# SwiGLU feed-forward on one core: the first loads in one line on SyncE, and two token chunks projected ahead of the third's transposes

## The chip, the core and the metric

The kernel runs on one core of a Trainium2 chip. The metric is the device time of one execution in microseconds (us), lower being better. A core has engines that run their own instruction streams side by side: TensorE (PE, matrix products), VectorE (DVE), ScalarE (ACT), GpSimd (POOL) and SyncE (SP), which here does nothing but issue transfers. Transfers between the device memory (HBM) and the on-chip memory are issued by SyncE and ScalarE, one queue each, and are carried by 16 DMA engines. Engines wait for one another, and for transfers, through semaphores.

## What is computed

```python
def reference(x, w_gate, w_up, w_down):
    g = _silu(x @ w_gate)
    u = x @ w_up
    return (g * u) @ w_down
```

`x` is 1 x 2048 x 640, `w_gate` and `w_up` are 640 x 1536, `w_down` is 1536 x 640, all bfloat16.

## The kernel before, in words

Tokens are worked on in four blocks of 512 (`S_BLK`), each of four chunks of 128. For each block the kernel forms the gate and up projections transposed, features on partitions: for each of the 12 slices of 128 features (`fc`) and for gate and up in turn, five matmuls (one per 128 of the 640 inputs) add up in a PSUM tile of 128 x 512 (`proj`, line 190). ScalarE applies silu to the gate tile, VectorE multiplies it with the up tile into `aT` (`gate`, line 208). Then the block is multiplied with `w_down` (lines 260 to 314) and stored.

The projections need `x` transposed (`xT`). For blocks 1 to 3 transposing DMAs bring it (`turn_x`). Block 0 can't wait for that: its four chunks x0 to x3 are loaded as they lie (`load_x`, line 83) and transposed by TensorE against an identity, five 128 x 128 transposes a chunk, and copied from PSUM into `xT` by VectorE, or by ScalarE and VectorE in two parts (`transpose_chunk`, line 178; `split`, line 224).

The weights come in column chunks, `W_CHUNKS` (line 44): feature slice 0, slice 1, slices 2 and 3, then 4 to 7 and 8 to 11 (`load_w`, line 80). A row of slice 0 is 256 bytes in memory. Lines 106 to 119 set the order of the first loads:

- SyncE: x0, x1, the last two fifths of gate slice 0, the last three of up slice 0, gate slice 1, x3, up slice 1, gate 2-3, up 2-3, and so on.
- ScalarE: x2, the first three fifths of gate slice 0, the first two of up slice 0, then the first activation (`silu_first`, line 114), with which its table is loaded.

A queue's issues go out in order, and an issue that waits holds up those behind it. The program uses eight completion semaphores for all these transfers, in turn; a transfer that takes one again waits for the transfer that had it before.

The order of TensorE's work at the start is written out in `head` (line 217): 18 filler matmuls (`warm`), transposes of chunks 0 and 2, two fillers, transposes of chunk 1, two fillers, then the projections of feature slices 0 and 1 over the first three chunks (`pg0`, `pu0`, `pg1`, `pu1` are gate and up of slices 0 and 1), with the transposes of chunk 3 before `pu1`, and last the four small projections of chunk 3. `outer_chunks` (line 200) picks chunks 0 and 2 out of a PSUM tile and of `xT`, so that one matmul of 256 columns covers both. `keep_order` holds TensorE, ScalarE, VectorE and SyncE to the written order. After the head the loop over blocks (line 247) goes on with feature slice 2 of block 0.

Of the kernel before, what the change touches and what calls it, by code (L numbers as in the profile page):

```python
# [10 lines left out]
def _body(  # L11
# [8 lines left out]
    nc = tc.nc  # L20
    P = nc.NUM_PARTITIONS
# [11 lines left out]
    KD = D // P  # L33
# [6 lines left out]
    N_WARM, N_GAP = 18, 2  # L40
# [3 lines left out]
    W_CHUNKS = [(0, 1), (1, 2), (2, 4), (4, 8), (8, 12)]  # L44
# [12 lines left out]
    wg_sb = consts.tile([P, KD, F], bf16)  # L57
    wu_sb = consts.tile([P, KD, F], bf16)
# [14 lines left out]
    wg_v = w_gate.rearrange("(kd p) f -> p kd f", p=P)  # L73
    wu_v = w_up.rearrange("(kd p) f -> p kd f", p=P)
    wd_v = w_down.rearrange("(kf p) d -> p kf d", p=P)

    def wslice(a, b):
        return slice(a * P, b * P)

    def load_w(eng, dst, src, a, b):  # L80
        eng.dma_start(out=dst[:, :, wslice(a, b)], in_=src[:, :, wslice(a, b)])

    def load_x(eng, c0, c1):
        eng.dma_start(out=x_sb[:, c0:c1, :], in_=x_v[:, c0:c1, :])  # L84
# [11 lines left out]
    def keep_order(engine):  # L96

        traced = [i for i in nc.cur_bb.bb.instructions if i.engine == engine]
        for a, b in zip(traced, traced[1:]):
            issue_order(a, b)  # L100
# [4 lines left out]

    load_x(nc.sync, 0, 1)
    load_x(nc.scalar, 2, 3)
    load_x(nc.sync, 1, 2)
    for dst, src, k in ((wg_sb, wg_v, 3), (wu_sb, wu_v, 2)):
        for eng, k0, k1 in ((nc.scalar, 0, k), (nc.sync, k, KD)):  # L110
            eng.dma_start(out=dst[:, k0:k1, wslice(0, 1)], in_=src[:, k0:k1, wslice(0, 1)])
    load_w(nc.sync, wg_sb, wg_v, *W_CHUNKS[1])
    load_x(nc.sync, 3, 4)
    nc.scalar.activation(silu_first[:], ones[:, 0:1], ACT.Silu)
# [12 lines left out]
    def turn_w(dst, src):  # L127
# [7 lines left out]
        out=x_row[:],  # L135
        in_=x2[S - T : S, :].rearrange("t d -> (t d)").partition_broadcast(P),
# [35 lines left out]
    def warm(n):  # L172
        for _ in range(n):
            nc.tensor.matmul(  # L174
                pw[:, 0:P], lhsT=ones[:], rhs=ones[:], start=True, stop=True
            )

    def transpose_chunk(c, parts):
        c_sl = slice(c * P, (c + 1) * P)
        for copy, tag, k0, k1 in parts:  # L180
            pt = psum.tile([P, k1 - k0, P], bf16, tag=tag, name="pt")
            for kd in range(k0, k1):
                nc.tensor.transpose(  # L183
                    out=pt[:, kd - k0, :],
                    in_=x_sb[:, c, kd * P : (kd + 1) * P],
                    identity=ident[:],
                )
            copy(out=xT[:, k0:k1, c_sl], in_=pt[:])  # L188

    def proj(ps, w_sb, fc, sb, c0, c1, cols=lambda ap: ap):  # L190
        for kd in range(KD):
            nc.tensor.matmul(  # L192
                cols(ps[:, c0:c1]),
                lhsT=w_sb[:, kd, fc * P : (fc + 1) * P],
                rhs=cols(xT[:, kd, sb * S_BLK + c0 : sb * S_BLK + c1]),
                start=(kd == 0),
                stop=(kd == KD - 1),
            )
# [4 lines left out]
    def gu_tiles():  # L203
        pg = psum.tile([P, S_BLK], f32, tag="gu", name="pg", bufs=4)
        pu = psum.tile([P, S_BLK], f32, tag="gu", name="pu", bufs=4)
        return pg, pu

    def gate(pg, pu, sb, fc, n_s):

        s0 = sb * S_BLK  # L210
        sg = work.tile([P, S_BLK], f32, name="sg")
        nc.scalar.activation(sg[:, 0:n_s], pg[:, 0:n_s], ACT.Silu)  # L212
        nc.vector.tensor_tensor(  # L213
            out=aT[:, fc, s0 : s0 + n_s], in0=sg[:, 0:n_s], in1=pu[:, 0:n_s], op=ALU.mult
        )

    def head():

        dve, act = nc.vector.tensor_copy, nc.scalar.copy
        split = [(act, "po_a", 0, 2), (dve, "po_b", 2, KD)]
        late = (SUB - 1) * P
        (pg0, pu0), (pg1, pu1) = gu_tiles(), gu_tiles()
        warm(N_WARM)
        transpose_chunk(0, [(dve, "po_a", 0, KD)])
        transpose_chunk(2, [(dve, "po_b", 0, KD)])
        warm(N_GAP)  # L230
        transpose_chunk(1, split)
        warm(N_GAP)
        proj(pg0, wg_sb, 0, 0, 0, late, outer_chunks)
        proj(pg0, wg_sb, 0, 0, P, 2 * P)
        proj(pu0, wu_sb, 0, 0, 0, late)
        proj(pg1, wg_sb, 1, 0, 0, late)
        transpose_chunk(3, split)
        proj(pu1, wu_sb, 1, 0, 0, late)
        for fc, pg, pu in ((0, pg0, pu0), (1, pg1, pu1)):
            proj(pg, wg_sb, fc, 0, late, S_BLK)  # L240
            proj(pu, wu_sb, fc, 0, late, S_BLK)
            gate(pg, pu, 0, fc, S_BLK)
        keep_order(mybir.EngineType.PE)
        keep_order(mybir.EngineType.Activation)

    head()
    for sb in range(NSB):
        n_s = S_BLK if sb < NSB - 1 else S_BLK - T
# [26 lines left out]
        for q in range(P // Q):  # L275
            nc.scalar.dma_start(
                out=out2[
                    sb * S_BLK : sb * S_BLK + n_t, DA + q * Q : DA + (q + 1) * Q
                ].rearrange("(i r) c -> r i c", r=Q),
                in_=ot_q[q * Q : (q + 1) * Q, :].rearrange("r (i c) -> r i c", c=Q),  # L280
# [110 lines left out]
def kernel(tc, *args):  # L391
    _body(tc, *args)
    tc.close()
    tc.compile()
    _trim(tc.nc)
# [30 lines left out]
```

## Time and profile before

| | us |
|---|---|
| median of 4 runs | 164.4 |
| lowest and highest | 164.17, 164.72 |
| the profiled execution: its own time | 164.72 |
| its span in the trace | 163.4 |
| TensorE busy in it (799 matmuls) | 160.3 |
| VectorE, ScalarE busy | 111.8, 42.6 |
| first matmul of feature slice 2, block 0 | 10.26 |

The first loads of the profiled execution, from the trace's issue rows (start of the issue, and us until the data have landed):

| transfer | queue | KB | issued | to landing |
|---|---|---|---|---|
| x0 | SyncE | 160 | 0.00 | 2.3 |
| x2 | ScalarE | 160 | 0.12 | 2.7 |
| x1 | SyncE | 160 | about 0.45 | 3.0 |
| gate slice 0, three fifths | ScalarE | 96 | 0.57 | 3.7 |
| gate slice 0, two fifths | SyncE | 64 | 0.91 | 3.3 |
| up slice 0, two fifths | ScalarE | 64 | 1.05 | 3.5 |
| up slice 0, three fifths | SyncE | 96 | 1.39 | 3.6 |
| gate slice 1 | SyncE | 160 | 1.90 | 4.0 |
| x3 | SyncE | 160 | 2.81 | 3.6 |
| up slice 1 | SyncE | 160 | 3.20 | 3.6 |
| gate slices 2-3 | SyncE | 320 | 4.31 | 5.9 |
| up slices 2-3 | SyncE | 320 | 4.72 | 6.5 |

All times in a trace count from the start of the span. A timeline line gives start, duration, engine, line of the kernel, what was done, the count, and in brackets how long the engine had been idle and what ended that. Matmuls run in a pipeline: a group's duration runs to the end of its last matmul, so the pace is read from start to start. The time of an execution is its span plus some 1.3 us around it.

### The profile page before, as it was taken

Reading aid. Unit: us, or ns where it says so; the run is one execution under the profiler, and the core shown is the slowest. Engines: PE = TensorE matmul, PEld = TensorE weight load, DVE = VectorE, ACT = ScalarE, POOL = GpSimd, SP = SyncE. Lnnn points to the kernel's source line nnn. Section 1 sums busy time; section 2 is a strip of 40 time slices with the busy share of each in tenths; the row PEclk is TensorE's granted clock in tenths of the full one; section 3 lists DMA queues with packets and bytes.
Section 4 is the critical chain, followed back from the end, with each engine's and each line's share of the span. In section 5 each row is a group of like instructions: output and inputs, shape, how many; then the busy total and the mean of one; then the engine's idle time right before and its main releaser. Section 6 shows DMA issues by size and latency. Waiting matters only on the chain.

```text
span 163.4 us, 2121 instructions
## 1 busy us (share of the span) xinstructions
PE 160.3 (98%) x799; PEld 76.8 (47%) x799; DVE 111.8 (68%) x251; ACT 42.6 (26%) x73; POOL 0.6 (0%) x6
## 2 busy tenths in 40 slices
PE   9989999999999999999999999999999999999994
PEld 8754444444444444444444444444444444445442
DVE  2133333399649999979919999979964999993000
ACT  3142222212142222212332222221214222222121
POOL 1000000000000000000000000000000000000000
DMA  7999999994149997002210000000420000000312
GB/s 202 246 308 353 363 234 246 226 234 65 65 107 178 230 178 147 0 0 26 72 64 0 4 0 0 2 0 0 64 68 32 0 0 0 0 4 0 51 37 72
DMA packets 42585, 15.86 MB, mean 97 GB/s; under 512 B 34512, under 2 KB 42448, under 8 KB 42576
## 3 DMA queue, kind: packets, MB, share of 16 engines
q1 hardware_dynamic: 33680, 14.88, 37.1%
q10 hardware_dynamic: 8896, 0.85, 3.8%
q8 instruction: 6, 0.10, 0.3%
q14 instruction: 3, 0.02, 0.1%
HBM read 7.21 MB, written 2.62 MB: 60 GB/s over the span
## 4 chain that ended last, share of the span: by engine, by line
PE 92%; DMA 6%; ACTq 0%; DVE 0%; issue 0%
PE pg L192 30%; PE pu L192 30%; PE po_a L288 25%; PE po_t L263 6%; DMA wg_sb<-in_w_gate_dram 6%; PE po_b L305 0%; ACTq L84 0%; DVE ot_b L313 0%
## 5 line engine op out<-in xcount | busy, mean ns | idle before, releaser
L192 PE MATMUL pg<-xT,wg_sb 128*128 128x512 bf16 (+4 forms) x255 | 60.4, 369 | 0.6 <-DMA wg_sb<-in_w_gate_dram 0.6
L192 PE MATMUL pu<-xT,wu_sb 128*128 128x512 bf16 (+3 forms) x250 | 59.9, 370 | 0.0
L213 DVE TENSOR_TENSOR aT<-sg,pu 128x512 bf16<-128x512 f32 (+1 forms) x48 | 32.7, 683 | 30.0 <-PE pu L192 28.6
L212 ACT ACTIVATE sg<-pg 128x512 f32<-128x512 f32 (+1 forms) x48 | 28.6, 596 | 68.2 <-PE pg L192 65.1
L288 PE MATMUL po_a<-wd_sb,aT 128*128 128x512 bf16 x192 | 42.1, 379 | 0.0
L145 DVE SCALAR_TENSOR_TENSOR prod<-wgT,x_row 128x640 f32<-128x640 bf16 x48 | 39.4, 821 | 1.1
L145 DVE SCALAR_TENSOR_TENSOR prod<-wuT,x_row 128x640 f32<-128x640 bf16 x48 | 39.4, 822 | 1.0
L192 PEld LDWEIGHTS <-wg_sb 128*128 128x128 bf16 x255 | 24.6, 99 | 28.3 <-DMA wg_sb<-in_w_gate_dram 0.8
L192 PEld LDWEIGHTS <-wu_sb 128*128 128x128 bf16 x250 | 24.0, 98 | 27.5 <-DMA wu_sb<-in_w_up_dram 0.2
L288 PEld LDWEIGHTS <-aT 128*128 128x128 bf16 x192 | 18.8, 98 | 22.6
L296 ACT CAST ot<-po_a 128x512 bf16<-128x512 f32 x16 | 9.4, 585 | 32.4 <-PE po_a L288 20.0
L263 PE MATMUL po_t<-aT,wd_sb 128*128 128x512 bf16 (+1 forms) x48 | 10.4, 366 | 0.0
L263 PEld LDWEIGHTS <-wd_sb 128*128 128x128 bf16 x48 | 4.7, 98 | 5.1
L313 DVE CAST ot_b<-po_b 128x128 bf16<-128x128 f32 x1 | 0.3, 292 | 9.9 <-PE po_b L305 9.9
L188 DVE COPY xT<-pt 128x640 bf16<-128x640 bf16 (+1 forms) x4 | 1.7, 425 | 6.1 <-PE pt L183 6.0
L272 ACT CAST ot_t<-po_t 128x512 bf16<-128x512 f32 (+1 forms) x4 | 2.2, 559 | 11.6 <-PE po_t L263 11.6
L145 DVE DVE_READ_ACCUMULATOR prod<-wuT,x_row 128x1 f32 x48 | 4.0, 83 | 0.0
L145 DVE DVE_READ_ACCUMULATOR prod<-wgT,x_row 128x1 f32 x48 | 3.9, 82 | 0.0
L274 DVE STREAM_TRANSPOSE ot_q<-ot_t 128x512 bf16<-128x512 bf16 (+1 forms) x4 | 2.7, 678 | 1.7 <-ACT ot_t L272 1.7
L174 PE MATMUL pw<-ones 128*128 128x128 bf16 x22 | 2.9, 311 | 0.4 <-DVE ones L104 0.4
L174 PEld LDWEIGHTS <-ones 128*128 128x128 bf16 x22 | 2.3, 144 | 0.4 <-DVE ones L104 0.4
L183 PE MATMUL pt<-ident,x_sb 128*128 128x128 bf16 x20 | 2.4, 289 | 0.0
(15 smaller groups left out, 7.2 us busy)
## 6 DMA issues: line engine op xcount, KB each, us to landing
out_dram<-ot SPq DMA_DIRECT2D x16, 128.0 KB, 1.7
wd_sb<-in_w_down_dram SPq DMA_DIRECT2D x1, 1920.0 KB, 12.8
wg_sb<-in_w_gate_dram SPq DMA_DIRECT2D x2, 640.0 KB, 7.7
wu_sb<-in_w_up_dram SPq DMA_DIRECT2D x2, 640.0 KB, 8.5
x_row<-in_x_dram SPq DMA_DIRECT2D x1, 640.0 KB, 5.1
x_sb<-in_x_dram SPq DMA_DIRECT2D x3, 160.0 KB, 3.0
out_dram<-ot_q ACTq DMA_DIRECT2D x12, 32.0 KB, 2.1
wg_sb<-in_w_gate_dram SPq DMA_DIRECT2D x1, 320.0 KB, 5.9
```

What stands on the lines that cost most here:

```text
L145: nc.vector.scalar_tensor_tensor(out=prod[:], in0=wT[:, fc, :], scalar=1.0, in1=x_row[:, t, :], op0=ALU.mult, op1=ALU.mult, accum_out=acc[ ...
L174: nc.tensor.matmul(pw[:, 0:P], lhsT=ones[:], rhs=ones[:], start=True, stop=True)
L183: nc.tensor.transpose(out=pt[:, kd - k0, :], in_=x_sb[:, c, kd * P : (kd + 1) * P], identity=ident[:],)
L188: copy(out=xT[:, k0:k1, c_sl], in_=pt[:])
L192: nc.tensor.matmul(cols(ps[:, c0:c1]), lhsT=w_sb[:, kd, fc * P : (fc + 1) * P], rhs=cols(xT[:, kd, sb * S_BLK + c0 : sb * S_BLK + c1]), st ...
L212: nc.scalar.activation(sg[:, 0:n_s], pg[:, 0:n_s], ACT.Silu)
L213: nc.vector.tensor_tensor(out=aT[:, fc, s0 : s0 + n_s], in0=sg[:, 0:n_s], in1=pu[:, 0:n_s], op=ALU.mult)
L263: nc.tensor.matmul(po_t[:], lhsT=wd_sb[:, kf, DA:D], rhs=aT[:, kf, sb * S_BLK : sb * S_BLK + n_t], start=(kf == 0), stop=(kf == KF - 1),)
L272: nc.scalar.copy(ot_t[:], po_t[:])
L274: nc.vector.transpose(out=ot_q[:], in_=ot_t[:])
L288: nc.tensor.matmul(po_a[:], lhsT=aT[:, kf, s0 : s0 + P], rhs=wd_sb[:, kf, 0:DA], start=(kf == 0), stop=(kf == KF - 1),)
L296: nc.scalar.copy(ot[:], po_a[:])
```

## The change

Gate slice 0 and up slice 0 are no longer divided between the two queues. SyncE issues x0, gate slice 0, x1, up slice 0, gate slice 1, x3, up slice 1, and so on, each as one transfer; ScalarE issues x2 alone. In `head` the projection of gate slice 0 over chunks 0 and 2 is put ahead of the transposes of chunk 1; up slice 0, which was one projection of 384 columns over chunks 0 to 2, becomes one over chunks 0 and 2 (256 columns) and one over chunk 1 (128 columns); and two of the filler matmuls go.

```diff
     load_x(nc.sync, 0, 1)
     load_x(nc.scalar, 2, 3)
+    load_w(nc.sync, wg_sb, wg_v, *W_CHUNKS[0])
     load_x(nc.sync, 1, 2)
-    for dst, src, k in ((wg_sb, wg_v, 3), (wu_sb, wu_v, 2)):
-        for eng, k0, k1 in ((nc.scalar, 0, k), (nc.sync, k, KD)):
-            eng.dma_start(out=dst[:, k0:k1, wslice(0, 1)], in_=src[:, k0:k1, wslice(0, 1)])
+    load_w(nc.sync, wu_sb, wu_v, *W_CHUNKS[0])
     load_w(nc.sync, wg_sb, wg_v, *W_CHUNKS[1])
     load_x(nc.sync, 3, 4)
     nc.scalar.activation(silu_first[:], ones[:, 0:1], ACT.Silu)
@@ -228,11 +227,11 @@
         transpose_chunk(0, [(dve, "po_a", 0, KD)])
         transpose_chunk(2, [(dve, "po_b", 0, KD)])
         warm(N_GAP)
+        proj(pg0, wg_sb, 0, 0, 0, late, outer_chunks)
         transpose_chunk(1, split)
-        warm(N_GAP)
-        proj(pg0, wg_sb, 0, 0, 0, late, outer_chunks)
+        proj(pu0, wu_sb, 0, 0, 0, late, outer_chunks)
         proj(pg0, wg_sb, 0, 0, P, 2 * P)
-        proj(pu0, wu_sb, 0, 0, 0, late)
+        proj(pu0, wu_sb, 0, 0, P, 2 * P)
         proj(pg1, wg_sb, 1, 0, 0, late)
         transpose_chunk(3, split)
         proj(pu1, wu_sb, 1, 0, 0, late)
```

## The prediction

> **What bounds the kernel now.** I read the page's chain first, then the chain in order of time, then the timeline of the first 12 us, SyncE's waits, the landings, and the DMA rate in half-microsecond windows. By the page TensorE is nearly all of it:
>
> ```profile
> PE 92%; DMA 6%; ACTq 0%; DVE 0%; issue 0%
> ```
>
> From 10.26 us on the chain is matmul groups of 1.08 us without a hole, and the change touches nothing of that. What can move is the moment at which this stream starts. The chain in order of time says what sets it:
>
> ```profile
> 0.57 3.73 DMA wg_sb<-in_w_gate_dram
> 4.29 0.02 issue
> 4.31 5.91 DMA wg_sb<-in_w_gate_dram
> 10.22 0.05 issue
> 10.26 1.25 PE pg L192 x5
> 11.52 1.08 PE pu L192 x5
> ```
>
> ScalarE's gate piece lands at 4.29; only then does SyncE issue the gate columns of chunks 2 and 3 (below: **gate 2-3**), which land 5.91 us later, at 10.22, and TensorE starts on them at 10.26. SyncE's wait is named here, with its total, count and longest:
>
> ```profile
> SPq L81 <- DMA wg_sb<-in_w_gate_dram: 0.7, 1, 0.7
> ```
>
> It is no data dependence: the program deals eight completion semaphores out in turn, and the eleventh transfer, gate 2-3, reuses that of the gate piece. The timeline of the head (start, duration, engine, line):
>
> ```profile
> 2.38 1.25 PE L183 MATMUL pt<-ident,x_sb 128*128 128x128 bf16 x10
> ...
> 3.13 1.03 DVE L188 COPY xT<-pt 128x640 bf16<-128x640 bf16 x2 [2.79 <-PE pt L183]
> ...
> 3.63 0.74 PE L183 MATMUL pt<-ident,x_sb 128*128 128x128 bf16 x5
> ...
> 4.17 0.42 PE L174 MATMUL pw<-ones 128*128 128x128 bf16 x2
> ...
> 4.38 1.45 PE L192 MATMUL pg<-xT,wg_sb 128*128 128x256 bf16 x10
> ...
> 5.66 0.98 PE L192 MATMUL pu<-xT,wu_sb 128*128 128x384 bf16 x5
> ...
> 7.29 0.44 PE L183 MATMUL pt<-ident,x_sb 128*128 128x128 bf16 x5
> ...
> 7.57 0.98 PE L192 MATMUL pu<-xT,wu_sb 128*128 128x384 bf16 x5
> 8.38 0.44 PE L192 MATMUL pg<-xT,wg_sb 128*128 128x128 bf16 x5
> 8.66 0.44 PE L192 MATMUL pu<-xT,wu_sb 128*128 128x128 bf16 x5
> ...
> 10.26 1.25 PE L192 MATMUL pg<-xT,wg_sb 128*128 128x512 bf16 x5 [0.60 <-DMA wg_sb<-in_w_gate_dram]
> ```
>
> Read starts against starts, since matmuls overlap. Five transposes take 0.54 us at 3.63 (to 4.17) but 0.28 at 7.29 (to 7.57): the array doubles its pace in between. Stepping through single matmuls, the 256-column ones from 4.38 are 0.213 us apart and the 128-column ones from 5.38 are 0.056 apart, so the step is at about 5.3. At full pace five matmuls cost 0.28 at 128 columns and 0.81 at 384. The last group starts at 9.22 and is through at 9.50; TensorE then stands until 10.26: **0.76 us is the most that the head's loads can be said to cost here.**
>
> **What the Trainium skill says.** "TensorE: Matmul & The Clock Gate", Part 1, has the array at half its clock until it has been busy for one window of about 3.4 us; the windows run freely, so the step falls differently in each run. The trace agrees on the factor (0.213 us for 256 columns); that the moment varies, one trace can't show. Part 4 of that page says that transposes do not count as busy in the same way; no run here shows it. "DMA: Bandwidth & Descriptors", section "Issuing engines are not separate DMA queues", says that a second issuing engine saves issue time only. The trace speaks against that for these 256-byte rows (the granted clock, the DMA share and the GB/s stand last):
>
> ```profile
> 3.00:3.50 0.50, 0.50 (x7) 0.50 (x6) 0.37 (x1) 0.08 (x1) 0.00 (x0) 1.00 1.18 262
> ...
> 4.00:4.50 0.50, 0.50 (x7) 0.49 (x6) 0.24 (x2) 0.37 (x1) 0.00 (x0) 1.00 0.86 191
> ```
>
> In the first window both queues carry weights, in the second nearly SyncE's alone.
>
> **The change, part by part.**
>
> *ScalarE loses two issues* (0.45 and 0.51 us). Its table load moves forward by that; its next work that anyone waits for is the copy of chunk 1, later than 4.09 now. Worth nothing.
>
> *SyncE's line.* Two gate and two up pieces become one transfer each, x1 moves behind the gate. By the issue rows, x 0.34 to 0.41 us, a 160 KB weight chunk 0.43 to 0.49, 0.05 between: x0 at 0, gate 0 at 0.46, x1 at 1.00, up 0 at 1.45, gate 1 at 1.99, x3 at 2.53, up 1 at 2.92, gate 2-3 at 3.4. There are now eight transfers ahead of gate 2-3, not ten, so it waits for the first one's semaphore, landed by 2.8: the 0.7 us wait goes, and gate 2-3 is issued 0.9 us earlier.
>
> *Does it land earlier?* One end: its 5.9 us move along, 3.4 + 5.9 = 9.3. The other: landing is set by the bytes ahead, which are the same. Two 160 KB chunks (164 kB) that shared two queues at 262 GB/s (0.63 us) now go through one at 191 (0.86): 2 x 0.23 = 0.46 late, so 10.7. Between lies what I expect: in the window 6.0 to 6.5 the DMA share falls to 0.69 with 161 GB/s, a hole just ahead of gate 2-3's data that an earlier issue fills; 0.3 to 0.5 us bought back against 0.46 lost, and a little more from the issue. I take 9.95, nearly the middle of 9.3 and 10.7.
>
> *The small loads.* By the packets' records data come in issue order; x1's 160 KB began at about 2.0 us, needs 0.5 at the 320 GB/s of its window, and x1 landed at 3.45, so 0.9 after its bulk. Gate 0 takes x1's place: 2.0 + 0.86 + 0.9 is 3.8 at worst. x1 follows at about 4.3, up 0 at 5.0 to 5.45. Gate 1, x3 and up 1 had the same bytes ahead before: 5.9, 6.4, 6.8, or 0.46 later.
>
> *TensorE's order.* Transposes of 0 and 2 and the two fillers end at 3.64 as now. The projection of chunks 0 and 2 then needs VectorE's second copy, done at 3.13 + 1.03 = 4.16, and gate 0 (3.8 at worst by the above). So TensorE stands from 3.64 to 4.20, where it now does chunk 1's transposes and fillers; that cover is gone, cost 0.56 us, not on top but inside the following account:
> pg0 of 0 and 2, slow clock, 5 x 0.213 = 1.07, to 5.27; chunk 1's transposes, now after the step, 0.28, to 5.55 (x1 is there); pu0 of 0 and 2, no such row at full pace, between 0.28 and 0.81, by columns 0.54, to 6.09 (up 0 is there); chunk 1's copies start near 5.74 and take 0.37 (ACT row at 4.09: 0.37), so pg0 of chunk 1 starts at 6.15, 0.06 of waiting; 0.28 and 0.28, to 6.71; pg1 0.81 to 7.52; transposes 0.28; pu1 0.81, to 8.61; four groups of 0.28, to 9.73.
> Splitting pu0 (five more matmuls and weight loads, two fillers fewer) costs 0.54 + 0.28 - 0.81 = 0.01. In sum TensorE is through at **9.73 instead of 9.50, 0.23 later**; the gate chunk 1, x3 and up 1 are wanted at 6.71, 7.52 and 7.80, with 0.5 us and more to spare.
>
> *Sum.* The stream starts at the later of 9.73 (TensorE) and 9.95 (gate 2-3) plus 0.04, so about 9.98 instead of 10.26: -0.28 us. Up 2-3 is wanted one group later, at 11.06; it landed at 11.22, one us after gate 2-3, and comes at 10.95 by the same step. Against the profiled execution (164.72: span 163.4 and 1.3 around it) that is **164.4**. The profiled one is the slowest of the four; their median is also 164.4, so I expect no visible change. About 0.33 us, 0.2%, is what a measurement of this kernel can tell from none: 164.07 to 164.73.
>
> **Rivals.**
> *Clean gain.* Gate 2-3 lands by 9.3 and the clock steps up before 4.2. Then pg0 costs 0.54, not 1.07, TensorE is through at 9.2, and the stream starts 1.06 earlier: 163.7; with only half of it 163.95. For it: the wait on the semaphore is real. Against: every byte ahead of gate 2-3 is still ahead, and the four runs never fell under 164.17.
> *The clock steps up late (slower).* Place: the new hole at 3.64 to 4.20. A window with 0.56 of 3.41 us idle is 84% busy, and if that doesn't count as busy the step waits one window more, to 8.7 us. Price: 3.41 us at half pace, 1.7 lost, TensorE through at 11.4, 165.9. It decides from a step at 6.35 us on (9.73 + half of 1.08 = 10.27, which is 164.73). For it: the kernel before has no hole there. Against: if transposes don't count, the window was little over half busy before as well and still counted.
> *One queue is slower.* The 0.46 us isn't bought back: gate 2-3 at 10.7, start 10.74, 165.2. For it: 262 against 191 GB/s. Against: the hole at 6.0 to 6.5.
> *It doesn't do what it says:* an order of release by the compiler in which the eight semaphores fall otherwise and the wait stays: 164.4 to 164.7.
>
> **Chances.** Even, 164.2 to 164.7: 0.40, and 0.02 for the change without effect. Clean gain 0.18. Late clock 0.20. One queue slower 0.20. So faster 0.18, same 0.42, slower 0.40. The range leaves out the better half of the gain and what of the late clock goes past one window, under 2 in 10: 163.8 to 165.9. The likeliest case alone: 164.1 to 164.7.
>
> **What would show it.** The start of the first 512-column group tells the sum: 9.98. The issue of gate 2-3 should stand near 3.4 with no wait for a weight piece; its landing separates 9.3, 9.95 and 10.7. A hole on TensorE from 3.64 to about 4.2, ended by VectorE's copy, not by gate 0's load. Transposes of chunk 1 at 0.28 us for five say that the clock had stepped up; at 0.54, and chunk 3's too, the late clock holds. I am wrong if gate 0 lands after 4.2, or if the first group starts outside 9.7 to 10.3.

## The result and the profile after

| | before | after |
|---|---|---|
| median | 164.23 us (56 runs, 163.47 to 165.40) | 164.59 us (35 runs, 164.19 to 166.12) |
| ratio | | **1.0027**, 95% interval 1.0014 to 1.0039 |
| the profiled execution, its span | 164.72, 163.4 | 164.38, 163.1 |

The change makes the kernel 0.27% slower, some 0.4 us. Forecast was no visible change. (A ratio here leaves out runs over 1.5% above their kernel's fastest, as five of the 18 of e1 below, and can then lie under what the medians say.) The two profiled executions alone would say the opposite: after is 0.34 us the faster one. Before was profiled in an execution longer than nine tenths of its 56 runs, after in one shorter than two thirds of its own. That is the first thing to keep in mind in reading on: in every trace of this study the time is 154.4 to 154.5 us (in one, 154.7) more than the start of the first 512-column group, so a run's time tells when its head was done: at 9.8 for the median of before, at 10.15 for that of after.

What the page of after gives by engine, in its chain of waits:

```profile
PE 95%; DMA 3%; SPq 1%; DVE 0%; issue 0%
```

The loads' share is 3%, before 6%. Followed in order of time (start, duration, what) the chain has another load in it, at another place:

```profile
1.48 4.28 DMA wu_sb<-in_w_up_dram
5.76 0.05 issue
5.81 0.72 PE pu L191 x5
...
9.83 0.28 PE pu L191 x5
10.11 1.09 PE pg L191 x5
```

Gate 2-3, on which the chain of before hung, is gone. **Up slice 0**, issued at 1.48, takes 4.28 us and is at 5.76 the last thing that the head waits for; what follows is matmuls without a hole, 4.14 us from 5.81 to the first 512-column group at 9.95. The timeline of after, with the two waits of TensorE in brackets:

```profile
2.60 1.25 PE L182 MATMUL pt<-ident,x_sb 128*128 128x128 bf16 x10
...
4.43 0.78 PE L191 MATMUL pg<-xT,wg_sb 128*128 128x256 bf16 x5 [0.37 <-DVE xT L187]
5.08 0.45 PE L182 MATMUL pt<-ident,x_sb 128*128 128x128 bf16 x5
5.81 0.72 PE L191 MATMUL pu<-xT,wu_sb 128*128 128x256 bf16 x5 [0.28 <-DMA wu_sb<-in_w_up_dram]
...
9.95 1.24 PE L191 MATMUL pg<-xT,wg_sb 128*128 128x512 bf16 x5
```

The hole ahead of the first projection is there and is ended by VectorE's copy, as forecast. The second, 0.45 us from 5.36 (5.08 + 0.28) to 5.81, was not forecast. Gate 2-3 is issued at 3.85 with no wait ahead of it and lands 4.9 us later, at 8.78, over a microsecond before it is wanted: the wait that the change removes is really removed, and brings nothing.

Why is up slice 0 late? The DMA rate in half-microsecond windows (clock, DMA share and GB/s stand last) has a gap in it in after, just behind gate slice 0:

```profile
2.50:3.00 0.50, 0.40 (x4) 0.40 (x5) 0.00 (x0) 0.00 (x0) 0.00 (x0) 1.00 1.27 282
3.00:3.50 0.50, 0.50 (x7) 0.45 (x6) 0.14 (x1) 0.00 (x0) 0.00 (x0) 1.00 1.23 137
3.50:4.00 0.50, 0.50 (x6) 0.40 (x4) 0.46 (x2) 0.00 (x0) 0.00 (x0) 1.00 0.47 153
```

Before moved 262 and 208 GB/s in the last two; the second of them:

```profile
3.50:4.00 0.50, 0.50 (x8) 0.50 (x6) 0.46 (x2) 0.00 (x0) 0.00 (x0) 1.00 0.94 208
```

The gap is one in what is moved. From 3.0 to 3.5 after's DMA share is still 1.23 (packets are under way, and slow), from 3.5 to 4.0 it is 0.47. SyncE had issued x1 by 1.43 and up slice 0 by 1.92, so the engines were not short of issued work.

### The profile page after: what moved, and what is told of

The parts are those of the page before. It is cut to its first block, busy times and chain, and to the rows that moved or that the text cites. A ratio compares the mean times of both kernels' runs of the same rounds, so it can differ in the third digit from the quotient of the medians.

```text
span 163.1 us, 2125 instructions
## 1 busy us (share of the span) xinstructions
PE 159.9 (98%) x802; PEld 76.3 (47%) x802; DVE 111.8 (69%) x251; ACT 42.6 (26%) x73; POOL 0.6 (0%) x6
## 4 chain that ended last, share of the span: by engine, by line
PE 95%; DMA 3%; SPq 1%; DVE 0%; issue 0%
PE pu L191 32%; PE pg L191 31%; PE po_a L287 25%; PE po_t L262 6%; DMA wu_sb<-in_w_up_dram 3%; SPq L84 1%; PE po_b L304 0%; SPq L81 0%; DVE ot_b L312 0%; PE pt L182 0%
## 5 line engine op out<-in xcount | busy, mean ns | idle before, releaser
L191 PE MATMUL pu<-xT,wu_sb 128*128 128x512 bf16 (+4 forms) x255 | 60.1, 366 | 0.3 <-DMA wu_sb<-in_w_up_dram 0.3
```

What stands on the lines that cost most here:

```text
L191: nc.tensor.matmul(cols(ps[:, c0:c1]), lhsT=w_sb[:, kd, fc * P : (fc + 1) * P], rhs=cols(xT[:, kd, sb * S_BLK + c0 : sb * S_BLK + c1]), st ...
```

## The theories

**Late loads:** with all weights of slice 0 and x1 in SyncE's one queue the DMA engines move little from 3 to 4 us, x1 and up slice 0 come late, TensorE waits. **Order:** it is TensorE's new order, with a split projection and a hole, that costs. **Clock:** the hole makes the array's full pace come a window late in some runs. And about the forecast's basis: **one-off**, the late gate 2-3 of before's trace is one execution's. The medians below stand beside these of before: 164.19 for the first four kernels, 164.22 for the second four, 164.16 for the last. Diffs are against the kernel before where nothing else is said.

## First four: the two halves, the hole, the other queue

**e1: the new loads under the old order.**

```diff
     load_x(nc.sync, 0, 1)
     load_x(nc.scalar, 2, 3)
+    load_w(nc.sync, wg_sb, wg_v, *W_CHUNKS[0])
     load_x(nc.sync, 1, 2)
-    for dst, src, k in ((wg_sb, wg_v, 3), (wu_sb, wu_v, 2)):
-        for eng, k0, k1 in ((nc.scalar, 0, k), (nc.sync, k, KD)):
-            eng.dma_start(out=dst[:, k0:k1, wslice(0, 1)], in_=src[:, k0:k1, wslice(0, 1)])
+    load_w(nc.sync, wu_sb, wu_v, *W_CHUNKS[0])
```

> The loads of the changed kernel with TensorE's old order. Late-loads theory (the up weights of slice 0 and x1 come late through one queue, and TensorE waits for them): x1 lands near 5.0 us, the old order wants it at 3.6 and the up weights at 5.7, so this is the worst of all, 1.0 us or more over the kernel before, 165.2. Order theory (the hole of 0.5 us on TensorE and the split projection cost, the loads don't): no more than 0.1 us over the kernel before.

Measured: 166.01 us median, ratio 1.0068 (1.0038 to 1.0099). The loads alone cost far more than the whole change. Its timeline:

```profile
4.97 0.71 PE L182 MATMUL pt<-ident,x_sb 128*128 128x128 bf16 x5 [0.90 <-DMA x_sb<-in_x_dram]
```

x1, which landed at about 3.5 in before, is there at 4.92. Against the order theory; and the new order is what hides most of it in the change. The loss is more than the late x1 explains: TensorE steps to full pace only at about 8 us in this trace, of which more below.

**e2: the old loads under the new order** (the diff of the change without its first hunk).

> The old loads with TensorE's new order. Late-loads theory: within 0.2 us of the kernel before, since every weight is there when it is wanted (up slice 0 by 5.0 us, wanted at 5.5). Order theory: all of the loss, 0.4 us over the kernel before.

Measured: 164.24, ratio 1.0016 (0.9991 to 1.0041). The median is that of before, the interval reaches from nothing to the whole loss, and 3 of 14 runs are at 165 or over: for the late loads, not decisive. The trace is of a good run: the first projection starts at 4.33 behind VectorE's copy, no load is waited for at up slice 0, and the stream starts at 9.41.

**e3: fillers in the hole of the changed kernel** (diff against the changed kernel).

```diff
         transpose_chunk(2, [(dve, "po_b", 0, KD)])
-        warm(N_GAP)
+        warm(N_GAP + 5)
         proj(pg0, wg_sb, 0, 0, 0, late, outer_chunks)
```

> The changed kernel with five more filler matmuls in the hole ahead of the first projection (7 in place of 2). Clock theory (the hole makes the array's pace step up late in part of the runs): 0.2 us or more under the changed kernel, and its slowest runs, 165 and over, go. Late-loads theory: the same as the changed kernel within 0.15 us, since the fillers hide no load.

Measured: 164.58, ratio 1.0022 (1.0004 to 1.0041). The changed kernel's median to 0.01 us. Its slowest runs are not gone: 3 of 22 are at 165.0 or over (8 of 35 in the changed kernel). In its trace the pace steps up near 5.5 us, later than in that of after, so that TensorE comes to up slice 0 without a wait:

```profile
5.38 0.55 PE L182 MATMUL pt<-ident,x_sb 128*128 128x128 bf16 x5
5.76 0.71 PE L191 MATMUL pu<-xT,wu_sb 128*128 128x256 bf16 x5
...
9.90 1.24 PE L191 MATMUL pg<-xT,wg_sb 128*128 128x512 bf16 x4
```

But up slice 0 had landed only at 5.68, so an earlier step could have brought no more than the 0.08 us between. So the hole is not what shifts the median.

**e4: up slice 0 on the other queue** (diff against the changed kernel).

```diff
-    load_w(nc.sync, wu_sb, wu_v, *W_CHUNKS[0])
+    load_w(nc.scalar, wu_sb, wu_v, *W_CHUNKS[0])
```

> The changed kernel with up slice 0 issued by ScalarE behind x2, in place of SyncE behind x1. Late-loads theory: up slice 0 lands about 1 us earlier (4.7), the wait for it goes, 0.25 to 0.4 us under the changed kernel. Order theory: no change against the changed kernel.

Measured: 164.42, ratio 1.0028 (1.0004 to 1.0052). By ratio no gain; but the runs fall apart into two groups, 17 from 163.86 to 165.18, half of them faster than the changed kernel's fastest (164.19), and 5 from 165.80 to 166.19. Up slice 0 landed at 4.94 and nobody waited for it. The first group is what the late-loads theory asks for, though no trace is of it. The trace is of the second group:

```profile
5.66 0.74 PE L182 MATMUL pt<-ident,x_sb 128*128 128x128 bf16 x5
...
7.79 0.74 PE L191 MATMUL pu<-xT,wu_sb 128*128 128x128 bf16 x5
8.32 1.25 PE L191 MATMUL pg<-xT,wg_sb 128*128 128x384 bf16 x5
9.42 0.44 PE L182 MATMUL pt<-ident,x_sb 128*128 128x128 bf16 x5
```

Five 128-column matmuls at 7.79 take 0.53 us, start to start, and at 9.42 take 0.28: the full pace came at about 8.9 us, not at 5.3 as in the trace of before, and half of the 3.6 us between was lost, 1.8. That is the late clock that the prediction had among its rivals, seen.

## Second four: before again, a hole by itself, both suspects gone, x1 on the other queue

**e5: the kernel before, unchanged.**

> The kernel before, unchanged, for a second trace. One-off theory (the late landing of gate 2-3 at 10.22 us, on which the sum was built, was one slow packet of one execution): gate 2-3 lands by 9 us and nobody waits for it; the first 512-column group starts where TensorE's own work ends, 9.0 to 10.3 us, by when the clock steps up; time as before. Rival (gate 2-3 holds the kernel before in most runs): it lands after 9.7 and TensorE waits again.

Measured: 164.21, ratio 1.0006 (0.9992 to 1.0020). Between the two expectations:

```profile
8.77 0.44 PE L192 MATMUL pu<-xT,wu_sb 128*128 128x128 bf16 x5
9.40 1.25 PE L192 MATMUL pg<-xT,wg_sb 128*128 128x512 bf16 x4 [0.18 <-DMA wg_sb<-in_w_gate_dram]
```

TensorE had stepped up at 3.6 us here, was through at 9.05 and did wait for gate 2-3, which landed at 9.35. But 9.35 is 0.9 us better than in the first trace. In the other traces with the same loads (e2, e6, e9, e12) it landed at 8.41, 9.37, 8.17 and 8.26, and no one waited. So of six traces with those loads two wait for gate 2-3, for 0.76 and 0.35 us, and four don't: the 0.76 us were real, and not typical. In how many of the runs it binds is not known. (This is the trace whose time is 154.7 us over that start: TensorE waited once more, for ScalarE, at 39.0.)

**e6: a hole and nothing else, in the kernel before.**

```diff
-    N_WARM, N_GAP = 18, 2
+    N_WARM, N_GAP = 13, 2
```

> The kernel before with 13 filler matmuls at the start in place of 18, so that TensorE stands some 0.5 us, from 1.8 to 2.4, ahead of the first transposes, and nothing else moves. Clock theory: in 15% of the runs or more the clock steps up a window late, 165.5 us and over, where the kernel before has almost none, and the median rises by 0.2 us or more. Rival (a hole of that size is harmless to the clock): as the kernel before within 0.15 us, tail included.

Measured: 164.39, ratio 1.0020 (0.9998 to 1.0042); 7 of 22 runs at 165.0 or over (before, in the 75 runs beside it: 2), but only 2 over 165.5, where 15% were expected. Toward the clock theory, and not yet a proof: the trace is of one of its faster runs and steps up at 5.3.

**e7: both suspects taken away** (the edits of e3 and e4 together).

> The changed kernel with up slice 0 on ScalarE's queue and the hole filled by five more fillers, so the two suspects taken away together. Clock theory: the cluster of runs near 166 us that up slice 0 on ScalarE alone left (5 of 22) goes, the median stays near 164.2 to 164.4. Rival (that cluster has another cause): it stays at about one run in five.

Measured: 164.20, ratio 1.0010 (0.9996 to 1.0024), slowest run 165.01. The group near 166 is gone with the hole filled. The changed kernel with these two edits can't be told from the kernel before. Its windows beside those of after:

```profile
3.00:3.50 0.50, 0.50 (x7) 0.46 (x6) 0.00 (x0) 0.00 (x0) 0.00 (x0) 1.00 1.26 290
3.50:4.00 0.50, 0.50 (x11) 0.50 (x10) 0.40 (x1) 0.00 (x0) 0.00 (x0) 1.00 1.19 280
```

290 and 280 GB/s in place of 137 and 153: with ScalarE's queue loaded as well the gap is closed. Up slice 0 landed at 5.15 (e3, which differs in its queue alone: 5.68).

**e8: x1 on the other queue, under the old order.**

```diff
-    load_x(nc.sync, 1, 2)
-    for dst, src, k in ((wg_sb, wg_v, 3), (wu_sb, wu_v, 2)):
-        for eng, k0, k1 in ((nc.scalar, 0, k), (nc.sync, k, KD)):
-            eng.dma_start(out=dst[:, k0:k1, wslice(0, 1)], in_=src[:, k0:k1, wslice(0, 1)])
+    load_x(nc.scalar, 1, 2)
+    load_w(nc.sync, wg_sb, wg_v, *W_CHUNKS[0])
+    load_w(nc.sync, wu_sb, wu_v, *W_CHUNKS[0])
```

> TensorE's old order; the two weight chunks of slice 0 undivided on SyncE, x1 behind x2 on ScalarE. Late-loads theory (x1 between two weight chunks of one queue stalls what is behind it): x1 lands by 3.6 us, gate slice 0 by 4, up slice 0 by 4.9, no wait ahead of the first 512-column group; the kernel before's time within 0.2 us. Rival (undivided weight chunks on one queue are late by themselves): up slice 0 after 5.5, 0.3 us or more over the kernel before.

Measured: 164.22, ratio 1.0022 (0.9999 to 1.0045), runs from 163.74 to 166.51, and the trace is of the longest of them. The time is as the late-loads theory has it, the landings are not: there is no gap in the rate (325 and 289 GB/s from 3 to 4 us), yet x1 lands at 4.88, not by 3.6, behind x2 on its own queue with gate slice 0 beside it. In these traces x1 came by 3.7 only where it stood ahead of gate slice 0. Here TensorE stood 1.0 us for it, and the pace stepped up after 9 us.

## Last four: the order alone, the line in another order, a candidate, a longer hole

**e9: old loads, new order, hole filled** (e2 with the edit of e3).

> The old loads with TensorE's new order, its hole filled by five more fillers. Theory of two causes (late loads through one queue, and the hole that delays the clock): both are gone, so within 0.15 us of the kernel before and no run at 165.3 us or over. Rival (the new order costs its 0.23 us of TensorE time by itself): 0.2 us or more over the kernel before.

Measured: 164.35 beside 164.16, ratio 1.0013 (0.9996 to 1.0029), slowest 165.16. Each expectation is inside the interval. The 0.23 us that the prediction worked out for the order (0.14%) fits best, but no cost at all is not excluded.

**e10: x1 behind up slice 0 in the one line, hole filled** (diff against e3).

```diff
     load_w(nc.sync, wg_sb, wg_v, *W_CHUNKS[0])
-    load_x(nc.sync, 1, 2)
     load_w(nc.sync, wu_sb, wu_v, *W_CHUNKS[0])
+    load_x(nc.sync, 1, 2)
```

> The changed kernel with the hole filled and x1 behind up slice 0 in SyncE's line. If one line is slow whatever its order: up slice 0 lands by 4.7 us but x1 only near 5.4, where the transposes of chunk 1 wait for it; as the changed kernel with the hole filled, 164.6. If x1 between two weight chunks was the special harm: x1 by 5.0, nobody waits, 164.2.

Measured: 164.87, ratio 1.0042 (1.0023 to 1.0060). One line is slow in this order as well, and slower than expected: up slice 0 landed at 5.45, x1 at 5.97, 0.75 and 0.57 us later than that. Its windows and its wait:

```profile
3.00:3.50 0.50, 0.50 (x8) 0.45 (x7) 0.08 (x1) 0.00 (x0) 0.00 (x0) 1.00 0.52 116
3.50:4.00 0.50, 0.50 (x10) 0.50 (x9) 0.50 (x2) 0.00 (x0) 0.00 (x0) 1.00 0.45 90
```

```profile
6.01 0.45 PE L182 MATMUL pt<-ident,x_sb 128*128 128x128 bf16 x5 [0.88 <-DMA x_sb<-in_x_dram]
```

The gap stands behind gate slice 0 here too, with a weight chunk next and not x1. So it isn't x1's transfer that makes it. It shows in all four traces in which ScalarE's queue has only x2 (after, e1, e3, e10: DMA share 0.47, 0.59, 0.47 and 0.45 from 3.5 to 4.0), and not in e4, e7 and e8 (1.15, 1.19, 1.26), where it carries a second transfer; nor in e11 below (1.29), where it does too.

**e11: a candidate,** undivided chunks on two queues under the old order, so that gate 2-3 is the ninth transfer and, as in the changed kernel, finds its semaphore free in time.

```diff
     load_x(nc.sync, 1, 2)
-    for dst, src, k in ((wg_sb, wg_v, 3), (wu_sb, wu_v, 2)):
-        for eng, k0, k1 in ((nc.scalar, 0, k), (nc.sync, k, KD)):
-            eng.dma_start(out=dst[:, k0:k1, wslice(0, 1)], in_=src[:, k0:k1, wslice(0, 1)])
+    load_w(nc.scalar, wu_sb, wu_v, *W_CHUNKS[0])
+    load_w(nc.sync, wg_sb, wg_v, *W_CHUNKS[0])
```

> A candidate: TensorE's old order; gate slice 0 undivided on SyncE behind x0 and x1, up slice 0 undivided on ScalarE behind x2. Two queues as before, but two transfers fewer, so that gate 2-3 waits for no semaphore. If gate 2-3 holds the fastest runs of the kernel before (landing at 9.35 in its second trace, TensorE ready at 9.06): it lands 0.5 us earlier, 0.1 to 0.2 us under the kernel before. If not, or if gate slice 0 whole on one queue lands after 4.5: no gain, up to 0.2 us over.

Measured: 164.40, ratio 1.0012 (0.9993 to 1.0030); no gain.

```profile
5.08 1.47 PE L191 MATMUL pg<-xT,wg_sb 128*128 128x256 bf16 x10 [0.33 <-DMA wg_sb<-in_w_gate_dram]
```

Gate 2-3 lands at 8.08, but gate slice 0 whole on one queue only at 5.03, against 4.29 in two parts in the first trace. No kernel of this study is faster than the kernel before.

**e12: a hole twice as long in the kernel before** (8 fillers in place of 18).

> The kernel before with 8 filler matmuls at the start in place of 18, a hole of about 1.1 us ahead of the first transposes, twice that of 13 fillers. Clock theory: late steps become common, a third of the runs or more at 165.0 us and over (7 of 22 with 13 fillers), and the mean rises by 0.5 us or more. Rival: the size of a hole ahead of the transposes doesn't matter, no more late runs than with 13.

Measured: 164.62 beside 164.16, mean 0.52 us over, ratio **1.0040** (1.0022 to 1.0059); 7 of 22 at 165.0 or over, just under the third that was expected and as many as in e6. The fastest run has moved too (163.97, before 163.34).

```profile
2.28 1.25 PE L183 MATMUL pt<-ident,x_sb 128*128 128x128 bf16 x10 [0.85 <-DMA x_sb<-in_x_dram]
...
5.88 1.61 PE L192 MATMUL pu<-xT,wu_sb 128*128 128x384 bf16 x5
...
8.14 0.44 PE L183 MATMUL pt<-ident,x_sb 128*128 128x128 bf16 x5
```

Idle time ahead of the transposes, in which no load was late and no work was waiting, costs 0.4%. The five 384-column matmuls at 5.88, through at full pace in 0.81 us, take 1.45. That such a hole costs time is shown by the 22 runs, and the trace shows where: the pace steps up at 7.2 us.

Over all traces, TensorE's idle time from 0.4 us to the first projection, added up, is 0.6 us or less in ten (before none, after 0.5, e6 0.4), and the first matmul at full pace comes between 3.5 and 6.1 us there. In the other four it is 0.7 to 1.0 us (e4, e12, e8, e1), and the first one comes at 8.9, 7.2, 9.4 and 8.2. Within the ten the idle time doesn't order the steps: before, with none, steps up at 5.4, after at 4.6. One trace of a kernel says nothing of how often.

## Why the prediction was wrong, point by point

**Two steps failed,** one on each side of the comparison. Forecast was 164.4 for both kernels; before has 164.23, 0.17 less, and after 164.59, 0.19 more.

**The view that it rested on: the step that failed for before.** "0.76 us is the most that the head's loads can be said to cost here": true of that execution, and taken for the kernel. Gate 2-3's landing at 10.22 was the latest of the six traces with those loads (8.17 to 10.22). The prediction said that this was the slowest of four runs, and took their median, 164.4, for the kernel's. A sum against that execution gave -0.28; the measured difference between the two profiled executions is -0.34, and between the medians +0.36.

**"The small loads": the step that failed for after.** It put up slice 0 at 5.0 to 5.45, 0.1 us or more ahead of its use, from the bytes ahead of it, priced at 191 GB/s. It landed at 5.76 (5.68 in e3): the one queue did not run at 191 but at 137 and 153 GB/s for a microsecond. The same step had x1 at 4.3; it landed at 5.03. It had gate slice 0 at 3.8 at worst, and that held: 3.63. The rival "one queue is slower" named the cause, but followed it to gate 2-3 (10.7; measured 8.78) and not to up slice 0, which is wanted first.

**Luck.** The stream was forecast to start at 9.98, and in the trace of after it starts at 9.95. That is two errors that cancel: gate 2-3, which was to set it, landed 1.2 us earlier than the 9.95 forecast, and up slice 0 held TensorE in its place. So neither of the prediction's own signs of being wrong came (gate slice 0 after 4.2, a start outside 9.7 to 10.3); both look at the changed kernel alone, and none at up slice 0.

**"Does it land earlier?"** The issue went from 4.31 to 3.85 (3.4 forecast: the issues of x1 and x3 took 0.52 and 0.81 us, not 0.41). Landing 8.78, under the better end of 9.3.

**TensorE's order.** Through at 9.73, by the prediction; measured 9.94, with 0.45 us of standing for up slice 0 and a start 0.22 later (x0 landed at 2.56, not 2.33), less 0.42 for a clock that stepped up at 4.6 (first projection 0.65, not 1.07). The hole, the copies of chunk 1 and the 0.81 and 0.28 us groups came as worked out. Of the order's 0.23 us the runs can say no more than that e9 has 0.13% (-0.04 to 0.29).

**The late clock.** Right as a mechanism (e4's trace: 8.9 us, 166.04; e12) and near in price (1.8 us for 1.7). In the changed kernel it is rare: 1 of 35 runs is over 165.5 us, and in the profiled one the pace steps up at 4.6 us in spite of the hole. In e4 5 of 22 runs are over 165.5, and with the hole filled (e7) none. Why e4 has more of them than the changed kernel is not settled; in its trace TensorE also stood 0.31 us for x0 ahead of the transposes.

**The clean gain** was mis-summed: its 1.06 us are TensorE's alone. With gate 2-3 at its 9.3 the stream could start at 9.34, 0.92 us earlier.

**So** the late loads are the likeliest cause of the 0.27%. With the hole filled in both, up slice 0 in SyncE's line gives 164.58 (e3, ratio 1.0022, its interval above 1), and on ScalarE's queue 164.20 (e7, 1.0010, which can't be told from 1). Filling the hole alone gives nothing back (e3); moving up slice 0 alone leaves the runs near 166 (e4). But the intervals of e3 and e7 overlap, and each stands beside other runs of before, so the cause is well supported and not proven, and how much of the loss the hole and the order hold is not settled at this size. Why the DMA engines move so little behind an undivided chunk of 256-byte rows in a lone queue is not settled either; nor whether x0 comes some 0.15 us later for having such a chunk next behind it, which the traces suggest (mean start of the transposes 2.65 us in seven, 2.49 in six).

## What to carry to other kernels

A wait seen in one profiled execution is not yet a cost of the kernel: compare that execution's time with the other runs, and profile twice before building a sum on it. Where a change moves loads between queues, follow each of them to its own first use, not only the one that the chain shows: here the next bound was up slice 0, the load with the least slack. And keep TensorE fed until its pace has stepped up, or idle time that costs nothing where it stands can be paid for later (e12).

## What had not been expected of the hardware

In two traces of the same program, the kernel before, the array's pace steps up at 5.4 and at 3.6 us, and TensorE is through with the head at 9.50 and at 9.05. In both gate 2-3 came later still, so how much of the run-to-run spread, 163.5 to 165.4, comes from this is not shown. And two queues moved the first loads faster than one, by closing a gap: 280 to 290 GB/s (e7) against 137 to 153 (after) between 3 and 4 us, although the Trainium skill ("DMA: Bandwidth & Descriptors", section "Issuing engines are not separate DMA queues") gives a second issuing engine no more than the issue time.
